# Low query products of two attention heads as pairs in the two halves of the array's rows, with another order of a tile's steps

## The chip, the cores and the metric

The kernel runs on one core of a Trainium2 chip. The metric is the device time of one execution in microseconds (us); the core's engines work side by side, each through its own list of instructions in a fixed order: TensorE (PE, whose loading of stationary operands is shown apart as PEld), VectorE (DVE), ScalarE (ACT), GpSimd (POOL) and SyncE (SP), which issues most transfers.

## What is computed

An attention layer, whose queries are means of neighbouring pairs, followed by two feed-forward layers:

```python
def _attn_ref(q, k, v):                       # B=2, H=8, S=1152, D=64, float32
    q_pool = q.reshape(B, H, S // 2, 2, D).mean(axis=3)
    scores = scale * np.matmul(q_pool, k.transpose(0, 1, 3, 2))
    scores = scores - np.max(scores, axis=-1, keepdims=True)
    attn = np.exp(scores)
    attn = attn / (np.sum(attn, axis=-1, keepdims=True) + 1e-09)
    return np.matmul(attn, v)
# x = attn_out as (B*S/2 = 1152 tokens, 512)
# first layer:  softplus(x @ w_in) @ w_out                 (d_ff 2048)
# second layer: rms norm, then (silu(xn @ w_gate) * (xn @ w_val)) @ w_out   (d_ff 1536)
```

Every product is worked out to nearly float32: an operand is split into a high part, rounded to the reduced format fp32r, and a low part, the rounded rest; the products high by high, high by low and low by high are summed in PSUM.

## The kernel before

**Attention.** Heads go in eight pairs (`pb`, 0 to 7), head A and head B. A pair has 576 queries for each head, in tiles of 128: four full tiles (`x` = 0 to 3) for each head and a rest of 64 queries for each, which share a fifth, mixed tile (`x` = 4). A *unit* is one tile of one head. For a unit `qk` (L457) writes the scores, 128 queries by 1152 keys, into three PSUM banks: `s` of head A lies in its own three banks, `s` of head B in another three, with one buffer each. The keys of a head, `kk`, hold the high part in 64 partitions and the low part in the other 64, and the queries stand in both halves: `qh` (`qhA`, `qhB`) the high part twice, `ql` the low part twice. So three matmuls of 384 columns with `qh` give high by high and high by low, three with `ql` give low by high (and low by low). A full tile of both heads takes 12 such steps; the mixed tile takes nine.

Then `softmax` (L484): DVE takes the row maxima (`nm`, L490), ACT the exponentials into `p`, with the row sums into `den` (L492). PE transposes `p` 128 by 128, four to a PSUM bank `t` (`flip`, L500, matmuls of L511; `flip_m`, L789, for the mixed tile); there are two such banks, used in turn. ACT or DVE copies them into `pt`. `av` (L519) multiplies `pt` by the values `v`, 18 products in float32 (36 matmuls of L532), head A into the lower 64 output partitions, head B into the upper ones, each with 64 columns of the array; the result goes through a `t` bank to `O`.

**The order on PE** is written out by hand. `turn` gives a tile's transposes as steps: T0 and T1 for head A (chunks 0 to 3 and 4 to 7), T2 and T3 for head B, T4 for the last chunk of both. A turn of tile `x` (L838 to L871) weaves them with the scores of tile `x + 1` and with `av` of the tile before: T0, scores A, T1, `av`, T2, T3, scores B, T4. The last turn of a pair weaves the mixed tile's transposes with the first scores of the next pair.

**The order on the other engines** is made by a planner (`Plan.run`, L148). It goes through all operations in order of time with a cost for each, chooses between the engines that an operation may run on, and lets an operation that is more urgent by over `WAIT` = 3.5 go first (L176). Every engine then works strictly through its list.

**Feed-forward.** `m1_h`, `m1_out`, `m2_in`, `m2_out` run over three blocks of 384 tokens, 12 matmuls for each 128 by 512 piece of a weight (L642 to L644). The weights come as float64 and are decoded on ACT, DVE and POOL (`decode`) beside the attention and the first block. `norm` (L734) spreads the row norms by three transposes (L740) into the unused columns of three score banks and copies them out. The results leave through copies and DMAs (`m2_out`, L769).

Of the kernel before, what the change touches and what calls it, by code (L numbers as in the profile page):

```python
# [12 lines left out]
F32 = mybir.dt.float32  # L13
# [7 lines left out]
P = 128  # L21
# [11 lines left out]
N = 384  # L33
# [178 lines left out]
def body(ctx: ExitStack, tc: tile.TileContext, kT, qT, v, w1, w1o, wg, wv, w2o, rg, outT):  # L212
# [244 lines left out]
    def qk(pb, x, h):  # L457
# [23 lines left out]
        op([("PE", 0.09 + MM * KB * len(todo))], go, r=r, w=[(sc, None)])  # L481
        softmax(pb, x, h)

    def softmax(pb, x, h):  # L484
# [12 lines left out]
    def tbank():  # L497
        return plan.ring("t", 2, lambda: ps.tile([P, 512], F32, tag="t", name="t", bufs=2))

    def flip(pb, x, todo):  # L500
# [12 lines left out]
        (h0, c0) = todo[0]  # L513
        out = (lambda: pt()[:, c0:c0 + n, h0, :]) if todo[-1][0] == h0 else (lambda: pt()[:, c0, :, :])
        op([act(n * P, False), dve(n * P, psum=True)],
           lambda e: copy(e, out(), t()[:, :n * P].rearrange("p (c q) -> p c q", c=n)),
           r=[(t, None)], w=[(pt, (h, c)) for h, c in todo])

    def av(pb, x):  # L519
        s = st[pb]  # L520
        pt = units[pb, x, 0]["pt"]
        t = tbank()
        n = P if x < NF else D
        spill = x == NF and pb < NP - 1
        if spill:
            s["bank"] = t

        def go(e):
            for c in range(CK):
                for h in range(2):  # L530
                    rhs = pt()[:, c, h, :] if x < NF else pt()[:, c, 0, h * D:h * D + D]
                    nc.tensor.matmul(t()[h * D:h * D + D, :n], lhsT=s["v"][h]()[:, c, :], rhs=rhs,  # L532
                                     start=(c == 0), stop=(c == CK - 1))
            if spill:
                nc.tensor.transpose(t()[:C, P:2 * P], s["den"](), ident)
        op([("PE", 0.1 + CK * 0.24 * n / P + 0.12 * spill)], go,
           r=[(pt, None), (s["v"][0], None), (s["v"][1], None)] + [(s["den"], None)] * spill, w=[(t, None)])
        o = s["O"]
        op([dve(n, psum=True), act(n, False)], lambda e: copy(e, o()[:, x * P:x * P + n], t()[:, :n]), r=[(t, None)], w=[(o, x)])

# [190 lines left out]
            banks["spare"] = [plan.buf(lambda: None) for _ in range(2)]  # L731
        return banks["spare"][m], None, lambda: b()[:, N:]

    def norm(t, acc):  # L734
        b = banks["spare"][1]
        sx = [banks["h"][c][0] for c in range(KB)]

        def go(e):
            for c in range(KB):
                nc.tensor.transpose(sx[c]()[:, N:], acc()[:, c * P:(c + 1) * P], ident)  # L740
        op([("PE", 0.4)], go, r=[(acc, None)], w=[(b, None), (banks["spare"][0], None)])
        rv = ring("k", "rs", [P, N])
        for c in range(KB):
            op([act(P, False), dve(P, psum=True)], lambda e, c=c: copy(e, rv()[:, c * P:(c + 1) * P], sx[c]()[:, N:]),
               r=[(b, None)], w=[(rv, c)])
        r = rv
        xh, xl = X[(0, 1, 0)[t]]
        for k in range(KC):
# [20 lines left out]
    def m2_out(i):  # L769
        n, j = divmod(i, J2)  # L770
        expand("w2o", j, gs.pop(i), j == 0, j == J2 - 1)
        if j == J2 - 1:
            for m in range(KC):
                b, part, view = banks["out"][m]
                ob = ring("k", "raw", [P, 2 * DM], F32, 2) if m % 2 else ring("k", "t0", [P, DM], F32, 2)
                op([act(N, False), dve(N, psum=True)], lambda e, view=view, ob=ob: copy(e, ob()[:, :N], view()), r=[(b, part)],
                   w=[(ob, None)])
                op([("SP", 0.9)], lambda e, m=m, n=n, ob=ob: nc.sync.dma_start(out=outT[m, :, n * N:(n + 1) * N], in_=ob()[:, :N]),
                   r=[(ob, None)], lat=2.2)

    def turn(pb, x):
        g = units[pb, x, 0]
# [6 lines left out]
    def flip_m(pb, c0, n):  # L789
# [2 lines left out]
            first["pt"] = ring("a", "pt", [P, CK, 2, P], F32, 2)  # L792
        pt, pr = first["pt"], first["p"]
        t = tbank()

        def go(e):
# [3 lines left out]
        op([("PE", 0.09 * n + 0.03)], go, r=[(pr, None)], w=[(t, None)])  # L800
# [31 lines left out]
    for o in st[0]["kh"].writers[None]:  # L832
        o.deps.add(units[0, 0, 0]["mx"])
    prep(1)
    prev = None
    for pb in range(NP):
        last = pb == NP - 1
        for x in range(NF + 1):  # L838
# [4 lines left out]
            if x < NF:  # L843
                T[0]()
                qk(pb, x + 1, 0)
                T[1]()
# [5 lines left out]
                T[2]()  # L852
                T[3]()
                if x < NF - 1:
                    qk(pb, x + 1, 1)
                T[4]()
            else:
                if not last:
                    qk(pb + 1, 0, 0)
                T[0]()  # L860
                T[1]()
                if not last:
                    qk(pb + 1, 0, 1)
                else:
                    make_banks(1, "h")
                    m1_h(0)
                T[2]()
                av(*prev)
                if last:
                    scales(pb)  # L870
# [13 lines left out]
    for i in range(n1):  # L884
# [6 lines left out]
        if t and j == 6:  # L891
            norm_rows(t - 1, acc[t - 1])
        if t and j == 8:
            norm(t - 1, acc[t - 1])
        if t == NBLK - 1:
            feed(2 * J1 + 2 * (j + 1))
    feed(len(pieces))
# [1 line left out]
    for i in range(n2):  # L899
        n, j = divmod(i, J2)  # L900
        if i + 1 < n2:
            m2_in(i + 1)
        m2_out(i)
        if i == 1:
            acc[2] = norm_sum(2)
        if i == 5:
            norm_rows(2, acc[2])
        if i == J2:
            norm(2, acc[2])
    for which, name in (("soft", "softplus"), ("silu", "silu_and_others")):  # L910
        before = {"soft": "exp", "silu": "soft"}[which]
        first = op([("ACT", 1.3)], lambda e, name=name: nc.scalar.preload_act_table_set(name))
# [58 lines left out]
```

## Time and profile before

| | |
|---|---|
| median of three runs | 690.83 us (690.43 to 691.46) |
| the profiled execution, its own time | 691.12 us |
| its span in the trace | 689.1 us |
| PE / PEld busy in the span | 678.2 us (98%) / 654.1 us (95%) |
| DVE / ACT / POOL busy | 440.5 us (64%) / 334.4 us (49%) / 107.2 us (16%) |
| attention | until about 259 us of the span |
| mean granted TensorE clock | 0.996 |

The profile is one execution. Times in it are counted from the start of the span. A busy time of PE covers a matmul from its issue to the end of its results, and matmuls follow each other long before that end, so the rate of PE is read from the starts of groups that follow each other, not from their lengths.

### The profile page before, as it was taken

How to read it: one execution, taken by the hardware profiler on the slowest of the kernel's cores; microseconds unless marked ns; L12 is line 12 of the kernel's file. 1: busy time of each engine (PE TensorE's matmuls, PEld its weight loads, DVE VectorE, ACT ScalarE, POOL GpSimd, SP SyncE). 2: the span in 40 equal slices, each digit the busy share in tenths (PEclk: the TensorE clock that was granted, in tenths of full speed). 3: DMA queues.
4: the chain of work that ended last, by engine and by line, in shares of the span. 5: the costliest groups of instructions: out<-in, count | busy, mean ns of one | idle time of the engine just before them, and what ended most of it. 6: DMA issues, size and time to landing. Idle time of an engine off the chain costs nothing.

```text
span 689.1 us, 12450 instructions
## 1 busy us (share of the span) xinstructions
PE 678.2 (98%) x5067; PEld 654.1 (95%) x5067; DVE 440.5 (64%) x759; ACT 334.4 (49%) x616; POOL 107.2 (16%) x121
## 2 busy tenths in 40 slices
PE   8999999999999999999999999999999999999997
PEld 7989988898899989999999999999999999999997
DVE  8867878887877889898324468888775422231222
ACT  4887887878787876564112333464541200010001
POOL 0542423524253111000000000011210000000000
PEclk9999999999999999999999999999999999999999
DMA  7545343333413214454000023342540100010001
GB/s 207 165 130 135 110 134 88 101 88 104 117 37 109 81 64 162 174 184 152 1 1 1 32 90 114 133 154 93 182 164 21 47 0 1 1 47 0 1 1 46
DMA packets 20709, 59.77 MB, mean 87 GB/s; under 512 B 3823, under 2 KB 6062, under 8 KB 20654
## 3 DMA queue, kind: packets, MB, share of 16 engines
q1 hardware_dynamic: 20286, 58.73, 26.6%
q8 instruction: 39, 0.64, 0.4%
q10 hardware_dynamic: 368, 0.26, 0.2%
q14 instruction: 16, 0.13, 0.1%
HBM read 56.59 MB, written 2.39 MB: 86 GB/s over the span
## 4 chain that ended last, share of the span: by engine, by line
PE 95%; DVE 2%; ACT 1%; DMA 1%; issue 0%; ACTq 0%; DVEq 0%
PE s L642 16%; PE s L644 15%; PE s L643 15%; PE s L476 12%; PE t L532 10%; PE t L511 9%; PE t L644 5%; PE t L643 5%; PE t L642 5%; PE t L798 1%; DVE nm L490 1%; DMA kr<-in_kT_dram 1%; ACT pt L257 0%; DVE pt L259 0%; DVE kh L259 0%
## 5 line engine op out<-in xcount | busy, mean ns | idle before, releaser
L642 PE MATMUL s<-x,w 128*128 128x384 f32 x348 | 117.4, 337 | 0.5 <-ACT rs L257 0.5
L644 PE MATMUL s<-x,w 128*128 128x384 f32 x348 | 116.7, 335 | 0.0
L643 PE MATMUL s<-x,w 128*128 128x384 f32 x348 | 116.7, 335 | 0.0
L490 DVE TENSOR_REDUCE nm<-s 128x1 f32<-128x1152 f32 x72 | 97.6, 1356 | 21.9 <-PE s L476 20.6
L492 ACT ACTIVATE p<-s,nm 128x1152 f32<-128x1152 f32 x72 | 88.3, 1226 | 14.9 <-DVE nm L490 13.5
L511 PE MATMUL t<-ident,p 128*128 128x128 f32 x576 | 85.6, 278 | 3.2 <-DVE O L259 1.1
L257 ACT COPY pt<-t 128x512 f32<-128x512 f32 (+2 forms) x140 | 73.0, 533 | 31.2 <-PE t L511 23.3
L764 ACT ACTIVATE g<-s 128x384 f32<-128x384 f32 x36 | 17.7, 492 | 137.6 <-PE s L644 137.6
L643 PE MATMUL s<-gl,w 128*128 128x384 f32 x243 | 81.5, 336 | 0.0
L642 PE MATMUL s<-gh,w 128*128 128x384 f32 x243 | 81.5, 335 | 0.0
L644 PE MATMUL s<-gh,w 128*128 128x384 f32 x243 | 81.5, 335 | 0.0
L511 PEld LDWEIGHTS t<-ident,p 128*128 128x128 f32 x576 | 65.2, 140 | 16.8 <-issue 5.3
L532 PE MATMUL t<-pt,v 128*64 128x128 f32 (+1 forms) x1440 | 80.1, 265 | 0.0
L532 PEld LDWEIGHTS t<-pt,v 128*64 128x64 f32 x1440 | 71.3, 137 | 7.3 <-issue 7.3
L642 PEld LDWEIGHTS s<-x,w 128*128 128x128 f32 x348 | 65.4, 188 | 1.0 <-ACT rs L257 0.8
L643 PEld LDWEIGHTS s<-x,w 128*128 128x128 f32 x348 | 65.4, 188 | 0.0
L644 PEld LDWEIGHTS s<-x,w 128*128 128x128 f32 x348 | 65.4, 188 | 0.0
L316 ACT ACTIVATE t<-raw 128x512 f32<-128x512 f32 x68 | 45.3, 672 | 18.6 <-DVE w L262 11.4
L262 DVE TENSOR_TENSOR gl<-g,gh 128x384 fp32r<-128x384 f32 x83 | 46.8, 564 | 7.7 <-ACT gh L257 5.6
L766 DVE TENSOR_TENSOR g<-g,t 128x384 f32<-128x384 f32 x18 | 10.0, 555 | 62.5 <-PE t L644 60.8
L664 ACT ACTIVATE g<-s 128x384 f32<-128x384 f32 x36 | 17.7, 492 | 66.0 <-PE s L644 62.9
L259 DVE CAST gh<-g 128x384 fp32r<-128x384 f32 x58 | 21.1, 364 | 43.5 <-PE t L644 39.3
(149 smaller groups left out, 1239.4 us busy)
## 6 DMA issues: line engine op xcount, KB each, us to landing
raw<-in_w_dram SPq DMA_DIRECT2D x16, 512.0 KB, 3.6
raw<-in_w1o_dram SPq DMA_DIRECT2D x16, 512.0 KB, 3.4
qr<-in_qT_dram SPq DMA_DIRECT2D x28, 288.0 KB, 4.0
raw<-in_wg_dram SPq DMA_DIRECT2D x12, 512.0 KB, 3.4
raw<-in_wv_dram SPq DMA_DIRECT2D x12, 512.0 KB, 3.5
raw<-in_w2o_dram SPq DMA_DIRECT2D x12, 512.0 KB, 3.4
v<-in_v_dram SPq DMA_DIRECT2D x16, 288.0 KB, 3.0
kr<-in_kT_dram SPq DMA_DIRECT2D x7, 576.0 KB, 3.9
```

Source lines behind the costliest of these rows:

```text
L257: nc.scalar.copy(out, in_)
L259: engines[e].tensor_copy(out, in_)
L262: engines[e].tensor_tensor(out=out, in0=in0, in1=in1, op=o)
L316: o = op([("ACT", 0.68)], lambda e: nc.scalar.activation(out=t0(), in_=word(1).bitcast(F32), scale=2.0 ** -112, **(dict(func=AF.Prelu, alp ...
L476: nc.tensor.matmul(sc()[:, c, :N], lhsT=q()[:, cut], rhs=k()[:, c * N:(c + 1) * N], start=(i == 0), stop=(i == len(todo) - 1))
L490: u["mx"] = op([dve(S, psum=True)], lambda e: nc.vector.tensor_reduce(out=nm(), in_=sc()[:, :, :N], axis=AX.XY, op=ALU.max, negate=True), ...
L492: o = op([("ACT", 1.42)], lambda e: nc.scalar.activation(out=pr(), in_=sc()[:, :, :N], func=AF.Exp, bias=nm(), accum_out=s["den"]()[:, col ...
L511: nc.tensor.transpose(t()[:, i * P:(i + 1) * P], pr[:, c * P:(c + 1) * P], ident)
L532: nc.tensor.matmul(t()[h * D:h * D + D, :n], lhsT=s["v"][h]()[:, c, :], rhs=rhs, start=(c == 0), stop=(c == CK - 1))
L642: nc.tensor.matmul(out, lhsT=w[:, 0, cols], rhs=hi, start=start, stop=False)
L643: nc.tensor.matmul(out, lhsT=w[:, 0, cols], rhs=lo, start=False, stop=False)
L644: nc.tensor.matmul(out, lhsT=w[:, 1, cols], rhs=hi, start=False, stop=stop)
```

## The change

The scores of a full tile are made in other steps. `high` issues the three matmuls with `qh` for one head. `low` then issues, for both heads together, six matmuls with 64 rows each: head A's `ql` with the high part of its keys in partitions 0 to 63, head B's in partitions 64 to 127, alternately; the low by low product is left out. Only the first tile of the first pair and the mixed tiles keep `qk`. The softmax of both heads is planned behind `low`. A table, `TURNS`, gives the order of a turn's steps for each `x`; T4 is put off into the next turn (`t4`).

Besides, `WAIT` goes from 3.5 to 2.0; the transpose of `den`, which stood behind `av` of the mixed tile, goes to the mixed tile's last transpose; `norm` is divided into `norm_turn` (transposes and their copies) and `norm`, and for the last block two of its three transposes go ahead of an `m2_out`; and the last result leaves as two halves, copied by ACT and DVE, with one DMA from ACT's queue and one from SP's. `flip` gets an option `halves` that no call uses.

```diff
-WAIT = 3.5
+WAIT = 2.0
+TURNS = ["T0 hA hB lo T1 T2 T3 av",
+         "T0 hA t4 hB T1 lo T2 av T3",
+         "T0 hA t4 hB T1 lo T2 av T3",
+         "T0 t4 hA T1 av T2 T3",
+         "hB T0 t4 hA lo T1 av T2"]
...
+    def high(pb, x, h):
...
+        def go(e):
+            for c in range(KB):
+                nc.tensor.matmul(sc()[:, c, :N], lhsT=q()[:, cut], rhs=k()[:, c * N:(c + 1) * N], start=True, stop=False)
+        op([("PE", 0.09 + MM * KB)], go, r=[(k, None), (q, "m0" if x == 0 else "m1")], w=[(sc, None)])
+
+    def low(pb, x):
...
+        def go(e):
+            for c in range(KB):
+                for h in range(2):
+                    r = slice(h * D, h * D + D)
+                    nc.tensor.matmul(sc[h]()[:, c, :N], lhsT=q[h]()[r, cut], rhs=k[h]()[r, c * N:(c + 1) * N],
+                                     start=False, stop=True)
+        op([("PE", 0.18 + MM * KB)], go, r=[(k[h], None) for h in range(2)] + [(q[h], "m0" if x == 0 else "m1") for h in range(2)],
+           w=[(b, None) for b in sc])
+        for h in range(2):
+            softmax(pb, x, h)
...
-    def norm(t, acc):
+    def norm_turn(t, acc, cs):
...
-            for c in range(KB):
+            for c in cs:
                 nc.tensor.transpose(sx[c]()[:, N:], acc()[:, c * P:(c + 1) * P], ident)
...
+                last = n == NBLK - 1 and m == KC - 1
+                both = [act(N, False), dve(N, psum=True)]
+                for c0, c1, opts, queue in ((0, N // 2, [act(N // 2, False)], "ACTQ"),
+                                            (N // 2, N, [dve(N // 2, psum=True)], "SP")) if last else ((0, N, both, "SP"),):
...
+            steps = {"av": avs if x < NF else lambda: av(*prev)}
+            for i, step in enumerate(T):
+                steps[f"T{i}"] = step
+            if x < NF - 1:
+                steps["hA"] = lambda: high(pb, x + 1, 0)
+                steps["hB"] = lambda: high(pb, x + 1, 1)
+                steps["lo"] = lambda: low(pb, x + 1)
+            elif x < NF:
+                steps["hA"] = lambda: qk(pb, NF, 0)
+            elif not last:
+                steps["hA"] = lambda: high(pb + 1, 0, 0)
+                steps["hB"] = lambda: high(pb + 1, 0, 1)
+                steps["lo"] = lambda: low(pb + 1, 0)
...
+        if i == J2:
+            norm_turn(2, acc[2], (0, 1))
         m2_out(i)
...
         if i == J2:
-            norm(2, acc[2])
+            norm_turn(2, acc[2], (2,))
+            norm(2)
```

What stands where now. First PE in the second pair, the turn of its tile 1 (before: `p_656` is that tile's head A, `p_711` its head B, `p_577` and `p_606` the tile before; the 18 products of `av` stand at the mark):

```order
L511 MATMUL t<-ident,p_577 128x128
L511 MATMUL t<-ident,p_606 128x128
L511 MATMUL t<-ident,p_656 128x128 x4
L476 MATMUL s<-kk_367,qhA_134 128x384 x3
L476 MATMUL s<-kk_367,qlA_365 128x384 x3
L511 MATMUL t<-ident,p_656 128x128 x4
...
L511 MATMUL t<-ident,p_711 128x128 x8
L476 MATMUL s<-kk_451,qhB_138 128x384 x3
L476 MATMUL s<-kk_451,qlB_514 128x384 x3
```

The same turn after the change (`p_673` is head A, `p_699` head B, `p_605` and `p_612` the tile before, `p_770` the next tile):

```order
L545 MATMUL t<-ident,p_673 128x128 x4
L498 MATMUL s<-kk_312,qhA_134 128x384 x3
L545 MATMUL t<-ident,p_605 128x128
L545 MATMUL t<-ident,p_612 128x128
L498 MATMUL s<-kk_320,qhB_138 128x384 x3
L545 MATMUL t<-ident,p_673 128x128 x4
L511 MATMUL s<-kk_312,qlA_400 128x384
L511 MATMUL s<-kk_320,qlB_488 128x384
...
L545 MATMUL t<-ident,p_699 128x128 x4
...
L545 MATMUL t<-ident,p_699 128x128 x4
L545 MATMUL t<-ident,p_770 128x128 x4
```

The scores of both heads are now complete at one point, with three or four steps between them and the next tile's T0; before, six steps stood between head A's scores and T0, and five between head B's and T2. T3 has moved behind `av`, and the next turn's T0 follows it directly.

Then DVE at the start of the program, behind the maxima of the very first unit: before (`nm_217` are the maxima of the first tile's head B, `nm_246` those of the second tile's head A; `y` is here the sum of head B's queries):

```order
L262 TENSOR_TENSOR qs<-qr 128x448
L453 TENSOR_SCALAR qhA_123<-qs 128x384
L490 TENSOR_REDUCE nm_217<-s 128x1
L393 SCALAR_TENSOR_TENSOR qlA_148<-qs,qhA_123 128x384
L262 TENSOR_TENSOR y<-p_142 128x448
L259 COPY pt<-t 128x4x128
L490 TENSOR_REDUCE nm_246<-s 128x1
L393 SCALAR_TENSOR_TENSOR qlB_180<-y,qhB_127 128x384
```

And after (`nm_210` is the first tile's head B, `nm_261` and `nm_275` the second tile's heads):

```order
L524 TENSOR_REDUCE nm_210<-s 128x1
L267 TENSOR_TENSOR qs<-qr 128x448
L267 TENSOR_TENSOR y<-p_142 128x448
L458 TENSOR_SCALAR qhA_123<-qs 128x384
L458 TENSOR_SCALAR qhB_127<-y 128x384
L398 SCALAR_TENSOR_TENSOR qlA_148<-qs,qhA_123 128x384
L398 SCALAR_TENSOR_TENSOR qlB_180<-y,qhB_127 128x384
L417 SCALAR_TENSOR_TENSOR qm_125<-qs,qhA_123 64x64
L524 TENSOR_REDUCE nm_261<-s 128x1
L524 TENSOR_REDUCE nm_275<-s 128x1
```

All four roundings of the remaining queries stand ahead of the second tile's maxima, and the maxima of the first tile's head B ahead of all of them. In the whole program 75 copies into `pt` stand on DVE, where 44 stood before, and 109 on ACT, where 140 stood.

## Rows read from the trace of the kernel before

**Rows 1.** The page: busy time; shares of the last chain; the transposes' group.

```profile
PE 678.2 (98%) x5067; PEld 654.1 (95%) x5067; DVE 440.5 (64%) x759; ACT 334.4 (49%) x616; POOL 107.2 (16%) x121
...
PE 95%; DVE 2%; ACT 1%; DMA 1%; issue 0%; ACTq 0%; DVEq 0%
...
L511 PE MATMUL t<-ident,p 128*128 128x128 f32 x576 | 85.6, 278 | 3.2 <-DVE O L259 1.1
```

**Rows 2.** Windows: stretch, length, busy us and instructions per engine, granted clock, DMA.

```profile
133.00:164.00 31.00, 30.68 (x329) 27.61 (x327) 24.99 (x34) 24.59 (x45) 10.75 (x12) 1.00 0.37 105
335.00:500.00 165.00, 165.00 (x958) 164.93 (x956) 106.91 (x209) 63.43 (x123) 11.12 (x9) 1.00 0.24 84
```

**Rows 3.** Groups of instructions by line and shape: count, busy us, mean ns, idle before.

```profile
L476 PE MATMUL s<-kk,qlB 128*128 128x384 f32 x96 | 22.5, 343 | 0.0
L476 PE MATMUL s<-kk,qlA 128*128 128x384 f32 x96 | 22.5, 343 | 0.0
```

**Rows 4.** Timeline, PE: start, length, line, operation, shape, count [idle before].

```profile
21.95 1.12 PE L511 MATMUL t<-ident,p 128*128 128x128 f32 x8
...
22.83 0.77 PE L476 MATMUL s<-kk,qhB 128*128 128x384 f32 x3
...
110.20 0.60 PE L511 MATMUL t<-ident,p 128*128 128x128 f32 x4
...
110.73 2.19 PE L532 MATMUL t<-pt,v 128*64 128x128 f32 x36
...
112.85 0.66 PE L511 MATMUL t<-ident,p 128*128 128x128 f32 x4
...
113.66 0.66 PE L511 MATMUL t<-ident,p 128*128 128x128 f32 x4 [0.16 <-DVE O L259]
```

**Rows 5.** Waits, PEld before `av` and before transposes: total us, times, longest.

```profile
PEld t L532 <- issue: 7.3, 40, 0.2
...
PEld t L511 <- issue: 5.3, 31, 0.2
```

**Rows 6.** Timeline, PE: the first matmuls in fp32r behind an `av`.

```profile
255.82 0.45 PE L642 MATMUL s<-x,w 128*128 128x384 f32 x1
...
256.11 0.34 PE L643 MATMUL s<-x,w 128*128 128x384 f32 x1
```

**Rows 7.** Timeline, DVE and ACT: maxima, exponentials, a copy out of a `t` bank.

```profile
110.47 1.36 DVE L490 TENSOR_REDUCE nm<-s 128x1 f32<-128x1152 f32 x1 [0.27 <-PE s L476]
...
111.91 1.23 ACT L492 ACTIVATE p<-s,nm 128x1152 f32<-128x1152 f32 x1
...
114.42 0.69 DVE L259 COPY pt<-t 128x512 f32<-128x512 f32 x1 [0.82 <-PE t L511]
```

**Rows 8.** Timeline, the start of the program.

```profile
10.49 1.16 PE L476 MATMUL s<-kk,qlB 128*128 128x384 f32 x3
...
11.04 0.62 DVE L262 TENSOR_TENSOR qs<-qr 128x448 f32<-128x448 f32 x1
...
11.69 0.36 DVE L453 TENSOR_SCALAR qhA<-qs 128x384 fp32r<-128x384 f32 x1
...
13.30 0.60 PE L511 MATMUL t<-ident,p 128*128 128x128 f32 x4
...
16.26 0.55 DVE L393 SCALAR_TENSOR_TENSOR qlB<-y,qhB 128x384 fp32r<-128x384 f32 x1
...
17.61 0.82 PE L511 MATMUL t<-ident,p 128*128 128x128 f32 x6
```

**Rows 9.** Timeline, PE: the norm of the last block.

```profile
546.61 0.34 PE L644 MATMUL s<-x,w 128*128 128x384 f32 x1
...
547.47 0.44 PE L642 MATMUL s<-x,w 128*128 128x384 f32 x1 [0.52 <-ACT rs L257]
```

**Rows 10.** Timeline, the end: the last copy and the last DMA's issue.

```profile
685.19 0.56 DVE L259 COPY raw<-t 128x384 f32<-128x384 f32 x1 [0.49 <-PE t L644]
...
685.78 0.33 SPq L778 DMA_DIRECT2D out_dram<-raw  x1
```

More of the change, by code (lines that the diff above doesn't have):

```diff
@@ L482, in qk @@
         softmax(pb, x, h)
+    def high(pb, x, h):
+        s = st[pb]
+        sc = units.setdefault((pb, x, h), {})["s"] = plan.ring("s" + "AB"[h], 1, lambda: score[h].tile(
+            [P, KB, 512], F32, tag="s" + "AB"[h], name="s", bufs=1))
+        cut = slice(x * P, (x + 1) * P)
+        q, k = s["q"][h][0], s["kk"][h]
+        def go(e):
[3 more added lines that the diff above has]
+    def low(pb, x):
+        s = st[pb]
+        sc = [units[pb, x, h]["s"] for h in range(2)]
+        cut = slice(x * P, (x + 1) * P)
+        q, k = [s["q"][h][1] for h in range(2)], s["kk"]
+        def go(e):
[8 more added lines that the diff above has]
+            softmax(pb, x, h)
     def softmax(pb, x, h):
@@ L513, in flip @@
         (h0, c0) = todo[0]
[L514 to L517, printed above, removed]
+        if todo[-1][0] != h0:
+            op([act(n * P, False), dve(n * P, psum=True)],
+               lambda e: copy(e, pt()[:, c0, :, :], t()[:, :n * P].rearrange("p (c q) -> p c q", c=n)),
+               r=[(t, None)], w=[(pt, (h, c)) for h, c in todo])
+            return
+        cuts = ((0, 2), (2, 4)) if halves else ((0, n),)
+        for i, j in cuts:
+            op([act((j - i) * P, False), dve((j - i) * P, psum=True)],
+               lambda e, i=i, j=j: copy(e, pt()[:, c0 + i:c0 + j, h0, :],
+                                        t()[:, i * P:j * P].rearrange("p (c q) -> p c q", c=j - i)),
+               r=[(t, None)], w=[(pt, hc) for hc in todo[i:j]])
     def av(pb, x):
@@ L523, in av @@
         n = P if x < NF else D
-        spill = x == NF and pb < NP - 1
-        if spill:
-            s["bank"] = t
         def go(e):
@@ L533, in go @@
                                      start=(c == 0), stop=(c == CK - 1))
[L534 to L537, printed above, removed]
+        op([("PE", 0.1 + CK * 0.24 * n / P)], go, r=[(pt, None), (s["v"][0], None), (s["v"][1], None)],
+           w=[(t, None)])
         o = s["O"]
@@ L775, in m2_out @@
                 ob = ring("k", "raw", [P, 2 * DM], F32, 2) if m % 2 else ring("k", "t0", [P, DM], F32, 2)
[L776 to L779, printed above, removed]
+                last = n == NBLK - 1 and m == KC - 1
+                both = [act(N, False), dve(N, psum=True)]
+                for c0, c1, opts, queue in ((0, N // 2, [act(N // 2, False)], "ACTQ"),
+                                            (N // 2, N, [dve(N // 2, psum=True)], "SP")) if last else ((0, N, both, "SP"),):
+                    op(opts, lambda e, view=view, ob=ob, c0=c0, c1=c1: copy(e, ob()[:, c0:c1], view()[:, c0:c1]),
+                       r=[(b, part)], w=[(ob, c0)])
+                    q = nc.sync if queue == "SP" else nc.scalar
+                    op([(queue, 0.9)], lambda e, m=m, n=n, ob=ob, c0=c0, c1=c1, q=q: q.dma_start(
+                        out=outT[m, :, n * N + c0:n * N + c1], in_=ob()[:, c0:c1]), r=[(ob, c0)], lat=2.2)
     def turn(pb, x):
@@ L794, in flip_m @@
         t = tbank()
+        spill = n == 1 and pb < NP - 1
+        den = st[pb]["den"]
+        if spill:
+            st[pb]["bank"] = t
         def go(e):
@@ L799, in go @@
                                     pr().rearrange("p b n -> p (b n)")[:, (c0 + i) * P:(c0 + i + 1) * P], ident)
-        op([("PE", 0.09 * n + 0.03)], go, r=[(pr, None)], w=[(t, None)])
+            if spill:
+                nc.tensor.transpose(t()[:C, P:2 * P], den(), ident)
+        op([("PE", 0.09 * (n + spill) + 0.03)], go, r=[(pr, None)] + [(den, None)] * spill, w=[(t, None)])
         op([act(n * P, False), dve(n * P, psum=True)],
@@ L851, in body @@
                     shift(pb - 1)
[L852 to L870, printed above, removed]
+            steps = {"av": avs if x < NF else lambda: av(*prev)}
[11 more added lines that the diff above has]
+                steps["lo"] = lambda: low(pb + 1, 0)
+            steps["t4"] = held
+            held = steps.pop("T4", None)
+            for name in TURNS[x].split():
+                if name == "T4":
+                    held, step = None, held
+                    step()
+                elif name == "t4":
+                    if steps["t4"]:
+                        steps["t4"]()
+                elif name in steps:
+                    steps[name]()
+            if x == NF and last:
+                make_banks(1, "h")
+                m1_h(0)
+                scales(pb)
             prev = (pb, x)
@@ L893, in body @@
         if t and j == 8:
-            norm(t - 1, acc[t - 1])
+            norm_turn(t - 1, acc[t - 1], (0, 1, 2))
+            norm(t - 1)
         if t == NBLK - 1:
```

22 lines of the change are left out of this document (12 added, 10 removed).

## Prediction

> **What bounds the kernel now.** Read the busy shares and the chain of waits first: PE is busy for 98% of the span and makes 95% of the chain that ended last; DVE has 64%, ACT 49% [rows 1]. Then the windows, since these are means over unlike stages. In the feed-forward stretch from 335 to 500 us PE issues 958 matmuls of 384 columns in 165.00 us, 0.172 us each, without a gap [rows 2]: the change touches nothing there, and nothing but fewer matmuls could help. In the attention, about 12 to 259 us, PE is busy for 30.68 of 31 us too, but DVE has 24.99 and ACT 24.59 [rows 2], about 80%: PE is the bound, with two engines close behind. So removed PE steps count in full until DVE and ACT, which get no less to do, fall behind.
>
> How much PE waits there is understated by its busy share. Groups of transposes show it: eight begin at 21.95 and the next group at 22.83, 0.11 us each; the four at 112.85 should last 0.44 and lead to the next at about 113.35 (their first load, behind `av`, is not ahead in time: 0.06), but that starts at 113.66. 0.31 us is lost where the row shows 0.16 idle [rows 4]. All transposes of L511 show 3.2 us [rows 1]; by that ratio some 6 us are lost in the attention, waiting for copies out of the two `t` banks.
>
> **The change part by part.** *Fewer steps.* `qlA` and `qlB` have 96 matmuls each, so 32 tiles [rows 3]; the first tile of pair 0 keeps the old form, 31 change. Six low steps take 6 x 0.172 = 1.03 us; three pairs, if the halves run side by side, 3 x 0.172 = 0.52. Saved: 0.52 us per tile, 16.0 us in all. No row shows a matmul on 64 rows. Nearest is `av`, whose matmuls pair two halves of the array's columns: 36 of 128 columns take 112.85 - 110.73 = 2.12 us, 0.118 a pair, while one float32 transpose of as many columns takes 0.11 [rows 4]. There two run in the time of one. I take that for the row halves; the other end is no overlap (a rival below).
>
> *What the halves cost.* The same rows show that a change of the array's form isn't free. The four transposes ahead of `av` take 0.53 us from their start to its start instead of 0.44 [rows 4]: 0.09 lost. PEld, which else loads ahead, stands idle at both edges of `av`: 7.3 us over 40 entries, 5.3 us over 31 exits, 0.18 and 0.17 each [rows 5]. And the first load behind such an edge can't hide: behind an `av` the first matmul in fp32r is followed after 0.29 us instead of 0.172, 0.12 lost [rows 6]. For `low` I count 0.18 + 0.17 = 0.35 us for both edges; the drains alone, 2 x 0.09 = 0.18, are the low end. At each of the 31 places `low` stands between steps of the full array, never beside `av`, so both edges are new. Net: 0.52 - 0.35 = 0.17 us a tile, **5.3 us** for 31; with the low end 0.34 and 10.5.
>
> *The new order of a tile.* Take times from the start of the last low matmul. Its results are there after 0.34 [rows 3]. Both heads' maxima now queue on DVE, 1.36 each, and the exponentials follow, 1.23 on ACT [rows 7]: head A's `p` is ready at 0.34 + 1.36 + 1.23, with the handovers about 3.05 us, head B's at 4.4. PE meanwhile has, in turns 1 and 2, the exit, T2, `av` and T3 (0.32 + 0.44 + 0.09 + 2.12 + 0.50 = 3.5 us) before T0 needs head A's, and T0, three high steps and t4 more (4.65) before hB overwrites head B's scores. Slack: 0.4 and 0.25 us. Turn 4 gives T0 at 3.25 and, since turn 0 has no t4 there, hB at 4.2: late by 0.2. Turn 0 has T1, T2, T3 and the half-length `av` of the mixed tile, 2.85: late by 0.2. In turn 0, too, T3 takes the bank of T1 with only T2 between, so it waits for a copy that needs about 0.7 us [rows 7] against 0.44: 0.3 to 0.4, which covers part of the lateness behind it. And T0 now stands behind `av` and T3 as T3 stood behind `av` and T2 (the 0.31 of rows 4). Together 0.8 to 1.0 us per pair, some 7 us, where 6 are lost now: **0.5 us more**, with bounds of 6 less (no wait left) and the rival below. Before, head A's scores had six steps of slack, so this is the part with least reserve. The move of `den`'s transpose to another step costs one transpose as before: nothing.
>
> *Start of the program.* In pair 0 hA and hB stand side by side and `low` needs both low parts, with no `av` to fill in. By the changed list DVE takes head B's maxima first (the scores end at 10.49 + 1.16 = 11.65, so to 13.0), then two sums (0.62), two high parts (0.36) and two low parts (0.55): `qlB` ends at 13.0 + 3.06 = 16.1 [rows 8]. PE, which does T0 at 13.30, waits for `qhA` until 14.6, and `low` runs at 16.1 to 17.0. Maxima and exponentials, 2.6 with handovers 2.7, bring the second tile's T0 to 19.7; before it began at 17.61 + 2 x 0.11 = 17.83 [rows 8]. That is 1.9 us, with t4 still to do 2.1, and 0.17 of it is the gain of one tile counted twice: **2.0 us lost**. If idle PE let its clock fall there, up to 2 us more; the clock is at full rate in the rows behind.
>
> *The norm of the last block.* PE stands from 546.61 to 547.47, 0.86 instead of 0.172, for three copies of the spread norms [rows 9]. Two of them now go ahead of 48 matmuls, and the third uses a bank that the next step doesn't: **0.69 us** gained. *The end.* The last copy takes 0.56 us on DVE before the last issue [rows 10]; half of it on either engine, with two issues side by side, gains at most 0.28: **0.2 us**. *The planner's* `WAIT` moves copies to DVE; what that may cost is in the rivals. Weight decoding stays ahead of PE (no wait of a matmul on a weight is among the gaps); I leave it at nothing, and up to 1 us if it slips.
>
> *The sum*, against the profiled execution's 691.12: - 5.3 + 0.5 + 2.0 - 0.7 - 0.2 = - 3.7, so 687.4. The median of the three runs is 0.29 below that execution: **687.1 us**, 0.5% faster.
>
> **The rivals.** *Cheap edges, fewer waits.* If only the drains count and the spread of T1, T2 and T3 over the turn leaves the copies enough time, the tiles give 10.5 and the waits 1 to 3 us less: 687.1 - 5.2 - 2 = about 680. For it: T1, hB, `low` and `av` now part the transposes in turns 1 and 2. Against it: the idle time of PEld at every edge.
>
> *The softmax queue decides; slower.* The bound moves to DVE in turns 0 to 2: two maxima in a row, and 31 more copies into `pt` by the changed lists, at 0.69 us [rows 7] some 21 us in 240, so its share there goes from 81% to almost 90%. Any DVE work ahead of the first maxima then delays both exponentials, and PE stands at T0 or hB. At 0.35 us more for each of 31 turns: 687.1 + 10.9 = 698.0. It decides from 0.12 us per turn, which uses up the 3.7. For it: slack of 0.25 us or less at hB. Against it: DVE's list puts the maxima ahead of most else, and PE's real edges give more time than the slack I counted.
>
> *Loads one after the other.* If the two halves' loads don't overlap, a pair takes 2 x 0.12 = 0.24 us by the load of [rows 6]; three and the edges 0.72 + 0.35 = 1.07, against 1.03: nothing is saved, 31 x 0.04 = 1.2 lost, and the time is 687.1 + 5.3 + 1.2 = 693.6. For it: `av`, 0.118 a pair with 64 columns loaded twice, doesn't exclude it. The Trainium skill, "TensorE: Matmul & The Clock Gate", section "LDWEIGHTS (loading the stationary operand)", makes the load last as long as its columns at 1.2 GHz, whatever the rows, 107 ns here by estimate, near the 0.12; it says in its part on packing that loads overlap where the row groups differ, and by that this rival falls.
>
> *No overlap.* Six low matmuls and new edges: 31 x 0.35 = 10.9 us lost instead of 5.3 gained, 687.1 + 16.2 = 703.3; the change would then not do what it says. `av`'s pairs write to different partitions, those of `low` to all 128 in two banks, so the row doesn't exclude it. The Trainium skill, "PSUM — Partial Sum Buffer", section "PSUM: the matmul accumulator", gives TensorE a single write port to PSUM; read strictly, the halves would take turns. No row of this kernel shows two results for the same partitions at once.
>
> **How the numbers follow.** A measurement here tells about 0.2%, 1.4 us, from no change: below 689.4 is faster, above 692.2 slower. Forecast (684 to 690): 0.50, of it 0.07 within 0.2%. Cheap edges: 0.22, faster. Softmax queue: 0.13, of it 0.03 within. Serial loads: 0.09, of it 0.02 within. No overlap: 0.06. So faster 0.43 + 0.22 = 0.65, same 0.12, slower 0.23. The range from 680 to 694 leaves out the case without overlap, most of the softmax queue and the lower edge of the cheap one, 0.2 in all.
>
> **What would show it.** Right: six low matmuls in about 0.52 us from the first start, in pairs some ns apart; PEld idle at some 62 new edges; 0.3 to 0.4 us less per tile than the matmuls alone promise; the second tile's T0 at about 19.7 us; a span of attention some 3 us shorter; no gap at the last norm. Wrong: low matmuls 0.12 or 0.17 us apart one by one; PE idle before T0 or hB in most turns with DVE's maxima as the releaser; a clock below full behind the start.

## The result and the profile after

The changed kernel takes 696.91 us (median of five runs, 696.6 to 697.16) against 690.69 (690.23 to 691.46): a ratio of 1.0089, 95% interval 1.0078 to 1.0101. It is 6.2 us slower, where 687.1 was predicted. The profiled execution took 697.09, its span 695.2 against 689.1.

The page, busy time and the transposes' group, which answer to [rows 1]:

```profile
PE 674.9 (97%) x5067; PEld 634.5 (91%) x5067; DVE 460.4 (66%) x802; ACT 323.5 (47%) x582; POOL 101.9 (15%) x113
...
L545 PE MATMUL t<-ident,p 128*128 128x128 f32 x576 | 90.0, 281 | 12.0 <-DVE O L264 5.5
```

PE has as many instructions as before and the transposes wait 12.0 us instead of 3.2. The same stretch of the attention as in [rows 2], PE first, and the three largest entries in the table of PE's waits (total us, times, longest):

```profile
133.00:164.00 31.00, 29.32 (x316) 24.30 (x315) 27.29 (x39) 23.54 (x40) 14.22 (x15) 1.00 0.41 112
```

```profile
PE t L545 <- DVE O L264: 5.5, 10, 1.4
PE t L545 <- ACT p L526: 2.6, 3, 1.0
PE t L545 <- ACT pt L262: 2.4, 9, 0.3
```

PE has 1.68 us without work in 31, where it had 0.32; DVE is at 88%, ACT at 76%. The granted clock is 1.00 in both stretches, so it plays no part there.

**Where the 6.2 us are.** The mixed tile's `av` (64 columns) comes once per pair. Its first and seventh start, before and then after:

```profile
44.24 1.27 PE L532 MATMUL t<-pt,v 128*64 128x64 f32 x36
...
227.46 1.27 PE L532 MATMUL t<-pt,v 128*64 128x64 f32 x36
```

```profile
48.43 1.27 PE L570 MATMUL t<-pt,v 128*64 128x64 f32 x36
...
236.01 1.27 PE L570 MATMUL t<-pt,v 128*64 128x64 f32 x36
```

Six pairs take 183.22 us before and 187.58 after: 30.54 and 31.26 each, 0.73 us lost per pair, 4.4 in six. In the first pair 4.19 us seem lost, but this `av` now stands at the end of its turn, 4.30 us behind T0 (169.19 to 173.49 below) instead of 2.07, so 2.23 of it is its place and 1.96 is lost. The eighth `av` of this kind starts 7.3 us later (258.13 before, 265.46 after), in the same place behind the first feed-forward products: 1.96 and 4.36 are these, and 1.0 falls in the last pair. The norm and the end give 1.0 back.

**The pairs.** PE in a turn of tile 1 (T1, `low`, T2, `av`):

```profile
177.87 0.60 PE L545 MATMUL t<-ident,p 128*128 128x128 f32 x4
178.40 0.44 PE L511 MATMUL s<-kk,qlA 64*128 64x384 f32 x1
178.40 0.44 PE L511 MATMUL s<-kk,qlB 64*128 64x384 f32 x1
178.68 0.33 PE L511 MATMUL s<-kk,qlA 64*128 64x384 f32 x1
...
178.85 0.33 PE L511 MATMUL s<-kk,qlA 64*128 64x384 f32 x1
...
179.12 0.66 PE L545 MATMUL t<-ident,p 128*128 128x128 f32 x4
179.71 2.19 PE L570 MATMUL t<-pt,v 128*64 128x128 f32 x36
```

The halves start together and a pair takes 0.17 us; the first is followed after 0.28. The edges cost 0.09 on the way in (four transposes last 0.53 instead of 0.44), 0.11 at the first pair, 0.09 to 0.10 on the way out (0.27 instead of 0.17) and 0.06 behind it (T2 to `av` 0.59): 0.35 to 0.36 in all, so `low` with its edges is worth 0.87 us against 1.03. That is the 0.17 us per tile of the prediction.

**The first tile's turn.** PE from `den`'s transpose of one pair through turn 0 (T0; hA, hB and `low` left out; T1 and T2; T3; `av`) to turn 1's T0:

```profile
168.80 0.27 PE L853 MATMUL t<-ident,den 128*9 128x128 f32 x1
169.19 0.63 PE L545 MATMUL t<-ident,p 128*128 128x128 f32 x4
...
171.52 1.09 PE L545 MATMUL t<-ident,p 128*128 128x128 f32 x8
172.91 0.66 PE L545 MATMUL t<-ident,p 128*128 128x128 f32 x4 [0.29 <-ACT pt L262]
173.49 1.27 PE L570 MATMUL t<-pt,v 128*64 128x64 f32 x36
176.12 0.63 PE L545 MATMUL t<-ident,p 128*128 128x128 f32 x4 [1.36 <-DVE O L264]
```

Three places lose time. T0 should follow `den` after 0.11 and follows after 0.39: 0.28, behind O's copy. T3 should follow 171.52 after 0.93 (0.06 for the load behind `low`, eight times 0.109) and follows after 1.39: 0.46, in the bank of T1, whose copy isn't done. And turn 1's T0 should follow the short `av` after 1.20 and follows after 2.63: 1.43. In seven pairs T3 loses 0.40 to 0.46 and turn 1's T0 0.55 to 1.43, 5.85 together. What DVE, ACT and POOL do meanwhile:

```profile
171.32 4.29 POOL L267 TENSOR_TENSOR kk<-kr,kk 64x384 fp32r<-64x384 f32 x4 [5.46 <-ACT kk L262]
171.36 1.37 DVE L267 TENSOR_TENSOR kk<-kr,kk 64x384 fp32r<-64x384 f32 x1
...
172.76 2.62 DVE L524 TENSOR_REDUCE nm<-s 128x1 f32<-128x1152 f32 x2
...
174.15 1.22 ACT L526 ACTIVATE p<-s,nm 128x1152 f32<-128x1152 f32 x1 [0.81 <-DVE nm L524]
...
175.30 0.68 DVE L264 COPY pt<-t 128x512 f32<-128x512 f32 x1
```

T0 takes T3's bank. T3's transposes are done at about 173.5, but its copy stands on DVE behind both maxima, which are one group from 172.76 to 175.38, and begins at 175.30. It ends at 175.98, and T0 starts at 176.12. ACT, which could have copied, stood idle for 0.81 us and then ran the exponential; head A's `p` is there at 175.37, 0.75 before T0 starts. So in this pair the bank came last. (The profile names the copy of O, which is the last event on DVE before. In the trace of experiment 2 T0 starts at 81.33, before that copy ends at 81.38, and 0.14 behind the end of T3's copy.) The bank didn't hold PE alone, though: without a wait T0 would have started at 174.69, so `p` was late as well. The maxima themselves began 1.17 us behind the end of `low` (171.25 + 0.34), since a subtraction for `kk` ran ahead of them.

In five of the seven pairs T3's copy stands on DVE behind both maxima, as here; T0 loses 1.06, 0.55, 1.43, 0.56 and 0.58 us. In the other two ACT makes the copy, ahead of head A's exponential, and T0 waits for `p` itself:

```profile
80.00 0.59 ACT L262 COPY pt<-t 128x512 f32<-128x512 f32 x1 [0.26 <-PE t L545]
80.48 1.23 ACT L526 ACTIVATE p<-s,nm 128x1152 f32<-128x1152 f32 x1
...
81.85 0.66 PE L545 MATMUL t<-ident,p 128*128 128x128 f32 x4 [0.69 <-ACT p L526]
```

Here T0 follows the end of the exponential, 81.71, by 0.14 and has lost 0.76; at 144.06 these are 0.15 and 0.91. So `p` was late in four pairs: in three because DVE had other work ahead of the maxima (in two of them the subtraction), in one behind T3's copy on ACT. By estimate, with 0.15 us from the end of the exponential to T0, `p` alone would have cost 0.46, 0.76, 0.91 and 0.83 us in these four and nothing in the other three: about 3.0 of the 5.85 us are the softmax, and 2.9 the bank. Where the softmax was prompt, the bank cost 0.55 to 0.58.

The waits of PE over 20 to 262 us are the distances between starts, less the distance that the same two kinds have without a wait (0.109 between transposes, 0.174 between matmuls of 384 columns, 1.20 over the short `av`). Where they are over 0.1 us (many smaller ones are left out) they come to 7.4 us before and 17.1 after. Of the 17.1, 11.0 are these three places; of the 7.4, 2.1 stood in the same turn, at T3, which waited for the copy of O. Elsewhere PE waits 6.1 us (1.05 of them in the last pair) against 5.3.

**Start, norm, end.** PE at the start (T0 of the second tile; T3 with T0 of the third), then at the last norm, then the last copies:

```profile
19.36 0.66 PE L545 MATMUL t<-ident,p 128*128 128x128 f32 x4 [1.04 <-ACT p L526]
...
25.16 1.21 PE L545 MATMUL t<-ident,p 128*128 128x128 f32 x8
```

```profile
551.70 0.34 PE L680 MATMUL t<-gh,w 128*128 128x384 f32 x1
...
551.90 0.43 PE L678 MATMUL s<-x,w 128*128 128x384 f32 x1
```

```profile
691.68 0.36 DVE L264 COPY raw<-t 128x192 f32<-128x192 f32 x1 [0.48 <-PE t L680]
...
692.08 0.32 ACT L262 COPY raw<-t 128x192 f32<-128x192 f32 x1 [0.39 <-DVE raw L264]
```

The second tile's T0 is at 19.36, near the 19.7 foreseen and 1.53 behind before [rows 8]. At the norm 0.20 us stand where 0.86 stood [rows 9]. The last two copies ran one after the other, ACT's waiting for DVE's, and still the span ends 3.52 us behind the first copy's start instead of 3.91 [rows 10].

### The profile page after: what moved, and what is told of

It is laid out like the page before. It is cut to its first block, busy times and chain, and to the rows that moved or that the text cites. A ratio compares the mean times of both kernels' runs of the same rounds, so it can differ in the third digit from the quotient of the medians.

```text
span 695.2 us, 12472 instructions
## 1 busy us (share of the span) xinstructions
PE 674.9 (97%) x5067; PEld 634.5 (91%) x5067; DVE 460.4 (66%) x802; ACT 323.5 (47%) x582; POOL 101.9 (15%) x113
## 4 chain that ended last, share of the span: by engine, by line
PE 65%; ACT 0%; DVE 0%; issue 0%
PE s L678 15%; PE s L680 15%; PE s L679 15%; PE t L680 5%; PE t L678 5%; PE t L679 5%; PE t L570 1%; PE t L545 1%; PE s L498 0%; PE s L748 0%; PE t L850 0%; PE s L481 0%; PE s L511 0%; ACT pt L262 0%; PE s L779 0%; DVE pt L264 0%
## 5 line engine op out<-in xcount | busy, mean ns | idle before, releaser
L545 PE MATMUL t<-ident,p 128*128 128x128 f32 x576 | 90.0, 281 | 12.0 <-DVE O L264 5.5
L524 DVE TENSOR_REDUCE nm<-s 128x1 f32<-128x1152 f32 x72 | 95.2, 1347 | 9.1 <-PE s L511 3.7
L545 PEld LDWEIGHTS t<-ident,p 128*128 128x128 f32 x576 | 63.3, 140 | 33.0 <-ACT p L526 11.2
L262 ACT COPY pt<-t 128x512 f32<-128x512 f32 (+2 forms) x109 | 56.7, 535 | 46.5 <-PE t L545 41.4
L264 DVE COPY pt<-t 128x512 f32<-128x512 f32 (+2 forms) x75 | 46.2, 625 | 18.7 <-PE t L545 12.6
```

What stands on the lines that cost most here:

```text
L262: nc.scalar.copy(out, in_)
L264: engines[e].tensor_copy(out, in_)
```

## The experiments

Each is compared with the kernel before in the same batch (medians 691.18 for 1 to 4, 690.84 for 5 to 8 and 690.99 for 9 to 12).

**1. The side edits alone, on the kernel before** (the norm's split, the last result in halves).

> The kernel before with two side edits alone: the last block's norm transposes divided (two ahead of an output step) and the last result in two halves on two queues; steps, orders and WAIT are those of before. The theory that the whole loss lies in the attention expects 690.7 less 0.8 for the norm (the 0.69 us and 0.11 us of late matmuls around it) and up to 0.4 for the end: about 689.6. The rival that these edits cost something elsewhere expects 690.7 or more.

690.82 us, ratio 0.9986 (0.9975 to 0.9998): 1.0 us gained by the ratio, 0.4 by the medians, where the two terms of the prediction give 0.9. So the other parts of the change cost about 7 us.

**2. The planner's constant.**

```diff
-WAIT = 2.0
+WAIT = 3.5
```

> The kernel after with WAIT back at 3.5, nothing else. If the planner's constant is what made DVE late (31 more copies into pt there), the time falls back by most of the 6.2 us, to 691 or below. If the order of the steps on PE does it, the time stays within 1.5 us of 696.9.

696.79, ratio 1.0073 (1.0054 to 1.0092); by the ratio at most some 2 us better, by the median the same. The constant isn't where the loss is.

**3. The pairs undone, everything else kept**: all low matmuls use 128 rows.

```diff
-                    nc.tensor.matmul(sc[h]()[:, c, :N], lhsT=q[h]()[r, cut], rhs=k[h]()[r, c * N:(c + 1) * N],
+                    nc.tensor.matmul(sc[h]()[:, c, :N], lhsT=q[h]()[:, cut], rhs=k[h]()[:, c * N:(c + 1) * N],
```

> The kernel after, every engine's list unchanged, but the six low matmuls of a tile run over all 128 rows, one after the other, as before the change (the low by low product is back). It takes the pairs away and keeps the order. If the pairs give the 0.17 us a tile that the rows of after show, the matmuls alone make it 31 x 0.17 = 5.3 us slower, 702.2; longer low steps also give the softmax more time, so waits may shrink and it may be as little as 2 us slower, 699. If the pairs are worthless or cost time, it is equal or faster than 696.9.

701.41, ratio 1.0139 (1.0122 to 1.0157): 4.5 us above the changed kernel, 3.5 by the ratios. The pairs are worth what was predicted, less some time that PE otherwise spends waiting: counted as above, the waits are 15.0 us here instead of 17.1. So the loss isn't in the pairs.

**4. T3's copy in turn 0 on ACT.** If T3's copy behind the maxima is the cause, another engine should free PE.

```diff
-            op([act((j - i) * P, False), dve((j - i) * P, psum=True)],
+            op([act((j - i) * P, False)] if only else [act((j - i) * P, False), dve((j - i) * P, psum=True)],
```

> The kernel after, but in the turn of a pair's first tile the copy of T3 out of its bank may only run on ACT (the planner makes the lists anew). In the trace of after this copy stands on DVE behind both maxima, and the next turn's T0 waits for its bank by 0.55 to 1.43 us in seven pairs, 5.9 us in all. If that queue is the cause, most of it goes: 2.5 to 4.5 us faster, about 693.5, with what is left set by the exponentials of head A. If T0 waits for the exponentials anyway, 696 or more.

701.7, ratio 1.0147 (1.0127 to 1.0166): 4.8 us worse, where 2.5 to 4.5 better was expected. Its trace, DVE, ACT and PE in one turn 0 (subtractions, maxima, T3's copy, turn 1's T0):

```profile
112.16 2.27 DVE L267 TENSOR_TENSOR kk<-kr,kk 64x384 fp32r<-64x384 f32 x2
...
114.46 2.62 DVE L524 TENSOR_REDUCE nm<-s 128x1 f32<-128x1152 f32 x2
...
117.06 0.58 ACT L262 COPY pt<-t 128x512 f32<-128x512 f32 x1
...
117.74 0.63 PE L546 MATMUL t<-ident,p 128*128 128x128 f32 x4 [1.41 <-ACT pt L262]
```

T0 follows the copy's end, 117.64, by 0.10: it is T3's bank that T0 waits for. But the planner gave DVE two subtractions ahead of the maxima, `low` being done at about 113.2, and the copy now stood behind the exponential, which ends (117.07) when both maxima do (117.08): on ACT it comes no earlier than on DVE. T0 lost 0.49 to 1.84 us in seven pairs, 7.2 in all; in the first of them the copy stood ahead of the exponential, and T0 waited for `p` (done at 53.20, T0 at 53.34). Another engine for this copy doesn't free PE by itself.

**5. T1 ahead of `low` in turn 0**: `"T0 hA hB T1 lo T2 T3 av"`, so that no three groups of transposes stand in a row.

> The kernel after with one entry of its order table changed: in the turn of a pair's first tile T1 goes ahead of the pairs (T0 hA hB T1 lo T2 T3 av instead of T0 hA hB lo T1 T2 T3 av). T3 then no longer waits for T1's copy (8 waits of about 0.5 us, 4.1 us in the trace of after), but one step less stands between the pairs and the next turn's T0. If the banks of the transposes set the loss of that turn, 2 to 4.5 us faster, about 693.5. If the chain of maxima and exponentials sets it, what T3 gains is waited for at T0, and the time stays within 1 us of 696.9.

699.5, ratio 1.0127 (1.0112 to 1.0143): worse by 2.6. T3's wait went; but `low` now ends later, with less behind it. The short `av`, the exponential of head A and T0:

```profile
176.45 1.27 PE L570 MATMUL t<-pt,v 128*64 128x64 f32 x36 [0.19 <-ACT pt L262]
...
176.91 1.22 ACT L526 ACTIVATE p<-s,nm 128x1152 f32<-128x1152 f32 x1
...
178.28 0.66 PE L545 MATMUL t<-ident,p 128*128 128x128 f32 x4 [0.56 <-ACT p L526]
```

Here T0 waits for `p` itself, as the prediction had it for this turn. In turn 0 the work behind `low` is too short for the softmax and, with one group more behind it, too dense for the banks: neither of the two places of T1 helps both.

**6. The hybrid: the scores of turn 0 in the old form, pairs in the other turns** (23 tiles). The turn isn't the old one in every step: T3 stands behind head B's scores, and `av` last.

```diff
-TURNS = ["T0 hA hB lo T1 T2 T3 av",
+TURNS = ["T0 QA T1 T2 QB T3 av",
...
+                steps["QA"] = lambda: qk(pb, x + 1, 0)
+                steps["QB"] = lambda: qk(pb, x + 1, 1)
```

> The kernel after with the first tile's turn alone taken back to twelve unpaired steps, head A's scores complete long before head B's (T0, six steps of A, T1, T2, six steps of B, T3, av); pairs stay in the other turns, 23 instead of 31. The theory that this turn holds the loss (11.8 of 19.0 us of waits of the transposes in after, and the late start of the program, 1.5 us) expects 1.4 us lost on the eight tiles and 8 to 10 us of waits and start gained: 688 to 690. The rival that pairs make both heads late in every turn, so that the loss is spread, expects 694 or more.

690.95, ratio 0.9998 (0.9989 to 1.0008), 1 us above the range expected. Eight turns of forty, changed in this way, give 6 us though eight tiles lose the gain of their pairs; the waits, counted as above, fall from 17.1 to 10.1 us. The short `av` and turn 1's T0, where 1.43 us were lost:

```profile
169.13 1.27 PE L570 MATMUL t<-pt,v 128*64 128x64 f32 x36
170.33 0.66 PE L545 MATMUL t<-ident,p 128*128 128x128 f32 x4
```

1.20 us apart, nothing lost, and so in all seven pairs. This settles the place: the loss is in the first tile's turn as the change made it, not in the pairs, their edges, the constant or the order of the other turns. What in that turn costs how much it doesn't part.

**7 and 8. The hybrid with T2 ahead of T1 in turn 4**, to take the wait behind `den`; and the same with the planner's PE costs closer to the trace (`low` 0.35 for 0.18, a transpose 0.11 for 0.09, and `av`).

```diff
-         "hB T0 t4 hA lo T1 av T2"]
+         "hB T0 t4 hA lo T2 T1 av"]
```

> The kernel of the run before, and in the mixed tile's turn the last transpose (with the transpose of the row sums) goes ahead of T1, so that T1 and av, and no longer a single short transpose, stand ahead of the next tile's T0. In after T0 waits there in seven pairs by 0.28 us for the copy of av's result. If that is so, 1.5 to 2 us faster than the run before, 686 to 688; if the bank that av now takes over after the row sums are read makes av wait, nothing.

> The kernel of the run before with the planner's costs on PE set to what the trace of after shows (pairs with their two edges 0.87 us instead of 0.70, a transpose 0.11 instead of 0.09, av 2.26 with its edges), so that the lists of DVE and ACT fit the real times; no step of PE moves. If lists made for a PE that is too fast put work in wrong places, 1 to 3 us faster than the run before; else within 1 us of it.

693.04, ratio 1.0032 (1.0019 to 1.0045), and 693.25, ratio 1.0034 (1.0022 to 1.0046): the first some 2 us slower than six, which its expectation hadn't foreseen, the second within 1 us of the first. The wait moved one step on, to `av` in the same bank, and grew: PE waits there seven times for ACT's copy, 5.0 us in all (5.3 in the second). Truer costs didn't help.

**9. The hybrid with the copy into `O` on DVE alone.**

```diff
-        op([dve(n, psum=True), act(n, False)], lambda e: copy(e, o()[:, x * P:x * P + n], t()[:, :n]), r=[(t, None)], w=[(o, x)])
+        op([dve(n, psum=True)], lambda e: copy(e, o()[:, x * P:x * P + n], t()[:, :n]), r=[(t, None)], w=[(o, x)])
```

> The hybrid (first tile's turn in the old form, pairs in the other turns), with one more edit: the copy of av's result into O may run on DVE alone. In the hybrid PE stood 1.15 us at 134.74 and again at 195.75, each time because that copy had been put on ACT behind an exponential. If those two waits are what keeps the hybrid from showing the gain of its 23 pairs, 2 x 1.15 = 2.3 us go: 688.6, clearly faster than before. If the copy only moves DVE's queue, so that PE waits elsewhere by as much, it stays at 690.5 to 691.

690.0, ratio 0.9987 (0.9978 to 0.9996): about 1 us of the 2.3. One long wait is left, with the same pattern as in turn 0, in the mixed tile's turn. Maxima, the copy of T1, and T2:

```profile
131.12 2.61 DVE L524 TENSOR_REDUCE nm<-s 128x1 f32<-128x1152 f32 x2
...
133.65 0.68 DVE L264 COPY pt<-t 128x512 f32<-128x512 f32 x1
...
134.38 0.33 PE L850 MATMUL t<-ident,p 128*128 128x128 f32 x1 [1.39 <-DVE pt L264]
```

**10. The start alone**: the changed kernel with the old form in its very first turn.

> The changed kernel with one turn of 40 in the old form: the very first, in which the low products of the program's second tile must wait for both heads' low parts. It measures the start term of the prediction by itself. By the prediction (2.0 lost) 696.9 - 2.0 = 694.9; by the trace of the changed kernel (the third tile's T0 about 1.5 later than before) 695.4. If the first pair's loss is taken back by waits in the turns behind it, 696.5 to 697.

696.5, ratio 1.0089 (1.0075 to 1.0102): 0.4 us by the medians, none by the ratio. Its trace, the first T0, and T3 with T0 of the third tile:

```profile
15.42 0.60 PE L545 MATMUL t<-ident,p 128*128 128x128 f32 x4
...
26.36 1.18 PE L545 MATMUL t<-ident,p 128*128 128x128 f32 x8
```

These two turns take 10.94 us, against 12.07 in the changed kernel (13.09 to 25.16): 1.1 us. Up to the eighth short `av` 1.25 us of it are there, so the later turns don't take it back. This profiled execution took 698.38 us, above its median: its first T0 came 2.3 us later, since the first keys did (first matmul at 7.31, not 6.09) and since the granted clock was 0.66 in the mean from 12 to 16 us, partly the lower level of 1.2 GHz, where the changed kernel had the full rate. The start is worth between nothing, by the times, and 1.1 us, by the trace; nearer these runs don't tell.

**11. Experiment 9 with turn 0 in eight alternating steps** from the second pair on: `"hA T0 lA T1 hB T2 lB T3 av"`, with `lA`, `lB` the unpaired low products of one head.

> The kernel with O's copy on DVE alone, and from the second pair on the first tile's turn in eight alternating steps: high scores A, T0, low scores A, T1, high B, T2, low B, T3, av, with the low scores unpaired. In the form before it T0 came directly behind the mixed tile's last transposes and waited 0.28 us for O's copy, seven times; now three matmuls stand there. If a t bank is what T0 waits for, 7 x 0.28 = 2.0 us go: 686.6. If the later exponential of head A takes it back (PE waits at the next T0 or at the next high scores of head B), 688 to 689.

690.31, ratio 0.999 (0.998 to 1.0), slower than both expectations. The wait behind `den` went, 2.0 us, but T0 of turn 1 waits again, in all seven pairs by 0.27 to 0.40, 2.6 us together, for T3's copy, this time on ACT behind the exponential:

```profile
170.44 0.66 PE L556 MATMUL t<-ident,p 128*128 128x128 f32 x4 [0.32 <-ACT pt L262]
```

**12. The same with the mixed tile's scores in two parts around T0** in turn 3.

```diff
-         "T0 t4 hA T1 av T2 T3",
+         "m0 T0 t4 m1 T1 av T2 T3",
```

> The same, and in the turn of tile 3 the mixed tile's scores in two parts: three matmuls ahead of T0, six behind t4. Before, T0 came behind av and T3 and waited 0.3 to 0.4 us for O's copy, in seven of eight pairs (rows like the one at 153.80). If three matmuls ahead of T0 cover it, 7 x 0.35 = 2.5 us go: 684.1 by the sum. If T1, which takes T0's bank, waits instead (only t4 and six matmuls, 1.25 us, stand between, against the 1.0 that a copy takes), or the mixed maxima are late, no change against the kernel without this edit.

687.29, ratio 0.9952 (0.9938 to 0.9966): 3.0 us faster than eleven (2.6 by the ratios) for the 2.5 expected of this edit, and faster than both kernels. The 684.1 had counted on eleven's 2.0 as well. T3, the first three score matmuls, and T0 with t4 follow each other without a wait:

```profile
178.07 0.66 PE L578 MATMUL t<-ident,p 128*128 128x128 f32 x4
178.56 0.80 PE L531 MATMUL s<-kk,qhA 128*128 128x384 f32 x3
179.19 0.82 PE L578 MATMUL t<-ident,p 128*128 128x128 f32 x6
```

So here a bank's wait was taken away by a step that needs no bank, put between.

## Why the prediction was wrong

**The pairs: right.** Two halves run side by side, 0.17 us a pair; the edges cost 0.35 as estimated. The third experiment measured 3.5 to 4.5 us for the term of 5.3, with 2 us less of waits beside it. The Trainium skill, "TensorEngine Tiling (Array Packing)", section "Key Properties", says that a change of tiling mode drains TensorE, and that different tiles load and multiply in parallel; the trace agrees, and puts the first at about 0.09 us on each side. The rivals of serial loads and of no overlap fall, and with the latter the reading by which the halves take turns at one write port: the six results for the same 128 partitions took 0.72 us from the first start to the next step, edges in it, not 1.03 and edges.

**Norm and the constant: right; the end: more than foreseen.** 0.66 and 0.39 us in the trace, 0.4 to 1.0 together by experiment 1, for 0.69 and 0.2 (0.28 at most); nothing for `WAIT`, by medians.

**The start: too large.** 2.0 us were given for it. The late low parts came as described, and T0 at 19.36, 1.53 later than before for the 1.9 foreseen; putting the old form back returned 1.1 in the trace and 0 to 0.4 by the times.

**The step that failed is the term of + 0.5 us for the new order of a tile.** The waits grew by 9.7 us, from 7.4 to 17.1. The prediction did name turn 0 as the turn with the least behind `low`, and its 0.3 to 0.4 for T3 in T1's bank measured 0.40 to 0.46. What it got wrong is T0 of turn 1: "late by 0.2", partly covered, where 0.55 to 1.43 us were lost in each of seven pairs, 5.85 together. Two things were missing. It let the maxima begin with the end of `low` and the exponential follow at once; in four pairs other work stood ahead of one or the other, and `p` came late. And it asked only when the exponential delivers `p`, not where the copy that frees T0's bank stands: in five pairs in DVE's order behind 2.6 us of maxima. By the estimate above each has about half of the 5.85 us. The 0.28 behind `den`, where T0 waits for the copy of O, is no new loss: T3 lost 0.2 to 0.3 to that copy in this turn before. In the other turns the waits changed little, 6.1 us against 5.3.

**The rival that came near, with another place.** "The softmax queue decides" gave 698.0. Its reason, DVE work ahead of the first maxima that makes the exponentials late for T0, is what the trace shows in three of the seven pairs. But it spread 0.35 us over all 31 turns; in fact the loss sits in one turn of five, at 1.3 to 2.2 us, and about half of T0's part comes from a copy into `pt` behind the maxima, which the rival didn't name. That its number lies 1.1 us from the measured one is luck. Its weight of 0.13 was too low: the prediction had counted 31 more copies on DVE and a share of almost 90%, and then took the order of DVE's list, maxima first, as a point against this rival, where that order makes the copy late.

What stays open: how much each of the three places in turn 0 would give alone, and how much the bank and the late exponential have of the third, which is an estimate from one trace. Experiments 4 and 5 tried to part them, and each moved the planner's other work as well; only changing the turn as a whole gave a clear answer. The delay of T4 and the move of `den`'s transpose weren't undone by themselves.

## What to carry to other kernels

When an order of steps is changed, follow for every step not only the data that it reads but the buffer that it takes, back to the instruction that frees it, and read what stands ahead of that instruction on its engine; with two buffers, as here, the copy's place in its engine's list cost more than its own 0.7 us. Do this for the shortest turn, not for the common one: here one turn of five lost more than the pairs in all the others gained. And when two producers are merged so that they end at one point, their consumers queue in one burst: small work behind that burst waits for all of it, and small work ahead of it makes all of it late.

## What was not expected of the hardware

A subtraction on DVE that begins just behind one on POOL lasts far longer than alone. In the changed kernel one begins at 171.36, 0.04 behind POOL's four (1.07 each, above), and takes 1.37 us; one that begins 0.02 ahead of POOL's takes 0.55:

```profile
108.61 0.55 DVE L267 TENSOR_TENSOR kk<-kr,kk 64x384 fp32r<-64x384 f32 x1
108.63 3.32 POOL L267 TENSOR_TENSOR kk<-kr,kk 64x384 fp32r<-64x384 f32 x3 [4.14 <-ACT kk L262]
```

In the twelfth experiment a rounding that takes 0.42 alone takes 1.63, and ends 0.28 behind the POOL instruction that had begun 0.08 ahead of it:

```profile
185.05 1.43 POOL L267 TENSOR_TENSOR y<-O,rdb 128x576 f32<-128x576 f32 x1
...
185.13 1.63 DVE L458 TENSOR_SCALAR qhB<-qs 128x512 fp32r<-128x512 f32 x1 [0.19 <-POOL qs L267]
```

It looks as if DVE waits until POOL's running instruction is done. The Trainium skill, "Advanced Engine Details and Errata", section "Mode Summary", says that the second SBUF port of VectorE is shared with GPSIMD, and that GPSIMD instructions and VectorE's instructions in two-port modes block each other. The rows look like such blocking, but they don't tell whether these instructions ran in such a mode, and no experiment here parted this. It matters since such work stood ahead of the maxima: the two pairs with a slow subtraction (140.15, 1.24 us, and 171.36) lost 0.91 and 1.43 us at turn 1's T0, two with a fast one (108.61 and 202.91, 0.55 each) 0.55 and 0.56. A third with a fast one (77.61, 0.55) lost 0.76, by T3's copy on ACT.
